# Gate's logits on VectorE instead of TensorE, for 17 of 18 token tiles

## The chip, the cores and the metric

One Trainium2 chip, of which one NeuronCore runs the program. The metric is the device time of one execution in microseconds (us). Kernel before: median 1043.26 us of three runs (1043.04 to 1044.56).

## The reference

Attention with a threshold under the row's maximum, then a dense ELU layer, then a mixture of experts with one expert for each token. All data are fp32. The change concerns the line that makes the logits.

```python
def _moe_ref(x, w_in, w_out):                       # x: 2304 tokens x 512, from the attention
    h = x @ w_in                                    # 2048 wide
    g = np.where(h > 0.0, h, np.exp(np.minimum(h, 0.0)) - 1.0)
    return g @ w_out                                # called x2 below
...
    logits = x @ w_gate + modality_bias[modality_id]     # x = x2; w_gate: 512 x 8
    e_idx = np.argmax(logits, axis=1)
    probs = softmax(logits)
    gate_w = probs[np.arange(N), e_idx]
    for e in range(E):                                   # 8 experts
        mask = e_idx == e
        out[mask] = gate_w[mask, None] * (np.maximum(x[mask] @ w1[e], 0.0) @ w2[e])
```

## The kernel before, in words

The program has three parts on one core. `Phase1` computes attention and, batch by batch, the ELU layer's first product; it writes g to memory (`gD`). `Phase2` computes that product for the last batch, unpacks `w_out` into `WB`, and then goes over 18 **token tiles** of 128 tokens (`tokens`, i = 0 to 17); this loop is where the change lies. `lead` starts the first expert there, and `Experts` runs all the others.

In both phases a planner (`Plan`) sets the order. Each step is `pl.op(engine, cost, due, function, deps, buffers)`; the planner simulates the engines with these costs, takes among the steps that are ready the one with the lowest due time, and so fixes one order of instructions for each engine. On the chip each engine keeps to that order: an instruction that waits holds up all that stand behind it. `STEP` is the distance of the due times of two tiles, in ns. The framework adds waits so that two engines aren't in the same PSUM tile at once.

One token tile i, before the change:

- `load`, `hi`, `lo`, twice (a half of 8 slices of g each): a DMA of 512 KB into `gr`, a cast on ScalarE (ACT) into `gs`, and on GpSimd (POOL) the rest `gs` = `gr` - cast. There are two `gs` buffers: a half's cast waits until PE is through with the half before the last.
- `mm`: 48 matmuls of 128x512 on TensorE (PE), 24 to a half, sum x2 in a PSUM tile `u`.
- `copy`: ACT copies x2 to `xrow`. `turn`: four PE transposes of `xrow` into the PSUM tile `xt`. `turned`: ACT copies that to `xw`. `logits`: `xw` times `w_gate` on PE, four matmuls in the source, each run as two.
- `top`: seven small VectorE (DVE) instructions, bias, maximum, one-hot `ohb`. `rank`: three small matmuls on PE count the earlier tokens of the same expert; they need `ohb`. `place`: eight DVE instructions make an address; `table`: an indirect DMA issued by POOL writes the token's number there. `neg`, `ex`, `gate`: DVE, ACT, DVE make the gate weight; `put` writes the row to memory.

After tile 8, `first` picks the fullest expert so far; `weights` then loads its eight pieces in turn through one staging buffer `stg`: DMA, cast on ACT, rest on POOL, into `WA`. After tile 14, `begun` makes the number `base`, which SP (the queue that issues the DMAs) loads; behind it in SP's order stands `idx` of `lead`, then POOL gathers 256 rows (`xg`), and PE turns them round (L829) inside tile 17.

Of the kernel before, what the change touches and what calls it, by code (L numbers as in the profile page):

```python
# [8 lines left out]
F32 = mybir.dt.float32  # L9
# [4 lines left out]
ALU = mybir.AluOpType  # L14
# [5 lines left out]
B, H, S, D = 4, 8, 576, 64  # L20
# [38 lines left out]
class Plan:  # L59
# [726 lines left out]


PREDICT, SNAP = 8, 14
STEP = 12700
EARLY = 128 * (PREDICT + 1)  # L790

BLOCKS = [TT] + [(EARLY // (k + 1) + (NT - EARLY) // k + 1 + 127) // 128 for k in range(1, E)]
# [263 lines left out]
class Phase2:  # L1056

    def __init__(self, tc, opt, ph, WA, WB, ident, w_out, mod, w_gate, bias, w1, w2, out, x2D, tabD):  # L1060
        self.tc, self.nc, self.opt, self.ph = tc, tc.nc, opt, ph
        self.ident, self.mod, self.w_gate, self.bias = ident, mod, w_gate, bias
        self.w1, self.w2, self.out, self.x2D, self.tabD = w1, w2, out, x2D, tabD
        self.WO = WB.rearrange("p s (k f) -> p s k f", k=FC)
        self.wsrc = w_out.bitcast(I32).rearrange("(k p) n -> p k n", p=128)
        self.gv = ph.gD.rearrange("k p s -> p k s")
        self.V = [WA, WB]
        self.T = ph.T
        self.pl = Plan(ph.pl)

    def pools(self, ctx, keep, xa, xb, tp):
        tc, pl = self.tc, self.pl
        self.xa, self.xb, self.tp = xa, xb, tp
        one = self.one = keep.enter_context(tc.tile_pool(name="k1", bufs=1))
        pool = lambda name, bufs, **k: ctx.enter_context(tc.tile_pool(name=name, bufs=bufs, reuse_waits="tile", **k))
        self.sm, self.wk = pool("msm", 3), pool("gwk", 2)
        self.pu, self.pc = pool("ps_u", 6, space=PSUM), pool("ps_c", 1, space=PSUM)
        for tag, n in dict(u=6, xt=1, pr=1, xw=2, eh=2, g=4, gr=2, gs=2, stg=1, xrow=3, ht=1).items():
            pl.ring(tag, n, tag in ("gs", "ht", "xw"))
        self.XT0 = one.tile([128, 2, KT, 256], F32R, name="xt0")  # L1080
        self.XG0 = one.tile([128, 2, XW], F32, name="xg0")
        self.IDX = [one.tile([128, 24], I32, name=f"idx{i}") for i in range(2)]
        self.GT = [one.tile([128, 2], F32, name=f"gt{i}") for i in range(2)]
# [96 lines left out]
    def gate_weights(self, d):  # L1180

        def load():
            self.wg = self.one.tile([128, KT, E], F32, name="wg")
            self.nc.sync.dma_start(self.wg, self.w_gate.rearrange("(k p) e -> p k e", p=128))

        self.k_wg = self.pl.dma(200, 1, d, load)

    def tokens(self, i, d):

        nc, pl, T, sm = self.nc, self.pl, self.T, self.sm  # L1190
        bU = pl.new("u")
        parts, ready = [], []
        for hf in range(2):
# [3 lines left out]
            n = 2 * i + hf  # L1197
# [21 lines left out]
        prev = None  # L1219
# [12 lines left out]
            prev = pl.op("PE", 1404, d + STEP // 2 * h, lambda f0=f0: mm(f0),  # L1232
                         [prev, *ready[2 * h:2 * h + 2]] + self.wdone[f0] + self.wdone[f0 + 1], [bU, parts[h]])
        self.k_mm = prev
        bX, bT, bW, bP = pl.new("xrow"), pl.new("xt"), pl.new("xw"), pl.new("pr")

        def copy():
            T["x", i] = self.wk.tile([128, XW], F32, name="xrow", tag="xrow", bufs=3)
# [6 lines left out]
                nc.tensor.transpose(T["xt"][:, 128 * k:128 * k + 128], T["x", i][:, 128 * k:128 * k + 128], self.ident)  # L1245

        def turned():
            if i < 2:
                T["xw", i] = self.xb.tile([128, KT, 128], F32, name="xw", tag=("xh", "xl")[i], bufs=1)
            nc.scalar.copy(T["xw", i % 2].rearrange("p k t -> p (k t)"), T["xt"])  # L1250

        def logits():
            for k in range(KT):
                nc.tensor.matmul(T["xt"][:, 0:E], T["xw", i % 2][:, k, :], self.wg[:, k, :], start=(k == 0), stop=(k == KT - 1))  # L1254

        def top():
            lg = T["lg", i] = sm.tile([128, E], F32, name="lg")
            nc.vector.tensor_tensor(lg, T["xt"][:, 0:E], self.bt[:, i, :], op=ALU.add)  # L1258
            mx = T["mx", i] = sm.tile([128, 4], F32, name="mx")
            nc.vector.tensor_reduce(mx[:, 0:1], lg, axis=AX.X, op=ALU.max)  # L1260
            t8 = sm.tile([128, E], F32, name="t8")
            nc.vector.scalar_tensor_tensor(t8, lg, mx[:, 0:1], self.d8, op0=ALU.is_ge, op1=ALU.mult)
            nc.vector.tensor_reduce(mx[:, 1:2], t8, axis=AX.X, op=ALU.max)
            oh = T["oh", i] = sm.tile([128, E], F32, name="oh")
            nc.vector.tensor_scalar(oh, self.d8, mx[:, 1:2], None, op0=ALU.is_equal)
            T["ohb", i] = sm.tile([128, E], BF16, name="ohb")
            nc.vector.tensor_copy(T["ohb", i], oh)
# [44 lines left out]
        if i == TT - 1:  # L1312
            d -= 15000
        k = pl.op("A", 478, d, copy, [prev], [bU, bX])
        k = pl.op("PE", 436, d + 700, turn, [k], [bX, bT])
        k = pl.op("A", 478, d + 1300, turned, [k] + (self.l1mm if i < 2 else []), [bT, bW])
        k = pl.op("PE", 880, d + 2000, logits, [k, self.k_wg], [bT, bW])
        kt = pl.op("D", 1200, d + 3000, top, [k, self.k_const, self.k_bias], [bT])
        kr = pl.op("PE", 60, d + 4300, rank, [kt, self.k_place], [bP])
        self.k_place = kp = pl.op("D", 1199, d + 4600, place, [kr], [bP])  # L1320
        self.k_table.append(pl.op("P", 1040, d + 5800, table, [kp, self.k_init], extra=2000))
# [324 lines left out]
```

## Time and profile before

| | |
|---|---|
| median of three runs | 1043.26 us |
| the profiled execution: its time, its span | 1040.67 us, 1038.7 us |
| PE busy | 987.1 us, 95% of the span |
| DVE busy | 633.5 us, 61% |
| ACT busy | 566.5 us, 55% |
| POOL busy | 472.2 us, 45% |
| PE clock granted | 0.988 of full speed |

How to read it: the shares are means over the whole program; the token tiles take about 532 to 770 us of the span. What an engine does there is read from the timeline and from tables of stretches below. Times within the profile are us from the start of the span.

### The profile page before, as it was taken

What the parts mean: (1) busy time and instruction counts of PE and PEld (TensorE: products, weight loads), DVE (VectorE), ACT (ScalarE), POOL (GpSimd) and SP (SyncE); (2) the same over time, 40 slices, a digit from 0 to 9 for tenths busy, and PEclk for the clock granted to TensorE, in tenths of its full rate; (3) what the DMA queues carried; (4) which work ended last, traced back from release to release, by engine and by line L of the source; (5) the groups of instructions that cost most, each with busy time, mean ns of one, the idle gap of its engine ahead of it and who ended that gap; (6) DMA issues with size and microseconds to landing.
All of it is one profiled execution on the core that took longest, in us unless ns stands there. A gap on an engine that the chain in (4) does not pass through costs nothing. (4 is left out here: it accounts for less than half of the span.)

```text
span 1038.7 us, 17784 instructions
## 1 busy us (share of the span) xinstructions
PE 987.1 (95%) x6241; PEld 864.3 (83%) x6241; DVE 633.5 (61%) x1574; ACT 566.5 (55%) x1183; POOL 472.2 (45%) x346
## 2 busy tenths in 40 slices
PE   8999899899999999998889999999999998999993
PEld 7666698899999999998778888877888897888982
DVE  6878899998989897856851222243444653464431
ACT  5777899899999999976762222333221211121000
POOL 3444787787667667541024444477523210211110
PEclk9999999999999999999999999999999999999997
DMA  5544454434424332116863333355312520441111
GB/s 174 152 121 128 118 152 132 123 117 118 131 88 123 99 111 70 59 64 199 227 211 113 105 104 103 114 153 172 112 41 83 200 65 24 141 122 53 41 44 25
DMA packets 107538, 117.75 MB, mean 113 GB/s; under 512 B 11920, under 2 KB 83872, under 8 KB 107426
## 3 DMA queue, kind: packets, MB, share of 16 engines
q1 hardware_dynamic: 102930, 104.00, 33.8%
q0 software_dynamic: 4496, 12.35, 3.9%
q8 instruction: 59, 0.97, 0.4%
q14 instruction: 53, 0.43, 0.1%
HBM read 80.36 MB, written 29.85 MB: 106 GB/s over the span
## 5 line engine op out<-in xcount | busy, mean ns | idle before, releaser
L1227 PE MATMUL u<-WB,gs 128*128 128x512 f32 x864 | 216.1, 402 | 3.7 <-POOL gs L1210 2.6
L1227 PEld LDWEIGHTS u<-WB,gs 128*128 128x128 f32 x864 | 158.4, 189 | 39.5 <-POOL gs L1210 3.7
L480 POOL TENSOR_TENSOR tl<-tf,th 128x512 fp32r<-128x512 f32 (+1 forms) x120 | 145.3, 1215 | 80.8 <-ACT tf L477 80.3
L715 PE MATMUL h<-xh,WA 128*128 128x288 f32 x768 | 172.4, 300 | 0.9 <-DVE g L734 0.5
L715 PEld LDWEIGHTS h<-xh,WA 128*128 128x128 f32 x768 | 128.8, 189 | 3.6 <-DVE g L734 1.9
L1210 POOL TENSOR_TENSOR gs<-gr,gs 128x1024 fp32r<-128x1024 f32 x36 | 87.1, 2420 | 95.2 <-ACT gs L1206 95.1
L419 DVE SCALAR_TENSOR_TENSOR p<-s,a,e 128x576 f32<-128x576 f32 x144 | 116.5, 813 | 19.5 <-ACT e L409 12.8
L397 DVE TENSOR_REDUCE a<-s 128x1 f32<-128x576 f32 x144 | 107.4, 753 | 16.4 <-PE s L386 14.1
L715 PE MATMUL h<-xl,WA 128*128 128x288 f32 x384 | 113.2, 295 | 0.0
L409 ACT ACTIVATE e<-s,a 128x576 f32<-128x576 f32 x144 | 106.8, 745 | 8.3 <-DVE a L397 6.4
L430 PE MATMUL h<-ident,p 128*128 128x128 f32 x576 | 87.8, 276 | 6.3 <-DVE p L419 4.9
L877 ACT CAST xtr<-px 128x512 fp32r<-128x512 f32 x16 | 9.4, 588 | 150.3 <-issue 85.2
L1258 DVE TENSOR_TENSOR lg<-xt,bt 128x8 f32<-128x8 f32 x18 | 3.0, 166 | 135.3 <-PE xt L1254 135.3
L820 POOL DMA_INDIRECT out<-o,idx x16 | 17.7, 1104 | 144.6 <-DVE o L932 101.3
L386 PE MATMUL s<-kh,QS 128*128 128x288 f32 x320 | 79.8, 331 | 1.4 <-DVE p L419 0.8
L430 PEld LDWEIGHTS h<-ident,p 128*128 128x128 f32 x576 | 68.8, 141 | 11.5 <-DVE p L419 4.7
L715 PEld LDWEIGHTS h<-xl,WA 128*128 128x128 f32 x384 | 72.6, 189 | 0.0
L386 PE MATMUL s<-kl,QS 128*128 128x288 f32 x320 | 69.1, 298 | 0.6 <-POOL kl L300 0.6
L1206 ACT CAST gs<-gr 128x1024 fp32r<-128x1024 f32 x36 | 37.8, 1049 | 56.5 <-issue 35.3
L471 ACT CAST th<-h 128x512 fp32r<-128x512 f32 (+1 forms) x120 | 64.0, 542 | 4.5 <-PE h L430 3.5
L477 ACT COPY tf<-h 128x512 f32<-128x512 f32 (+1 forms) x120 | 64.6, 546 | 1.4
L715 PE MATMUL u<-xh,WA 128*128 128x288 f32 x256 | 55.6, 306 | 8.6 <-DVE g L734 8.3
(207 smaller groups left out, 2083.7 us busy)
## 6 DMA issues: line engine op xcount, KB each, us to landing
gD<-g SPq DMA_DIRECT2D x128, 144.0 KB
gr<-gD SPq DMA_DIRECT2D x36, 512.0 KB
stg<-w SPq DMA_DIRECT2D x24, 512.0 KB
kr<-kP SPq DMA_DIRECT2D x30, 288.0 KB
w<-w_in SPq DMA_DIRECT2D x16, 512.0 KB
gr<-w_out SPq DMA_DIRECT2D x16, 512.0 KB
VR<-v SPq DMA_DIRECT2D x16, 320.0 KB
x2D<-xrow SPq DMA_DIRECT2D x18, 256.5 KB
```

The costliest lines, as they stand in the source:

```text
L386: nc.tensor.matmul(s[:, hf, 0:288], q, k[:, 288 * hf:288 * hf + 288], start=(m == 0), stop=(m == len(mm) - 1))
L397: nc.vector.tensor_reduce(T["a", i][:, 0:1], T["s", i][:, :, 0:288], axis=AX.XY, op=ALU.max, negate=True)
L409: nc.scalar.activation(e, T["s", i][:, :, 0:288], AF.Exp, bias=T["a", i][:, 0:1])
L419: nc.vector.scalar_tensor_tensor(p, T["s", i][:, :, 0:288], T["a", i][:, 1:2], T["e", i], op0=ALU.is_ge, op1=ALU.mult, accum_out=T["sums", ...
L430: nc.tensor.transpose(tp[:, 128 * c:128 * c + 128], pf[:, 128 * c:128 * c + 128], self.ident)
L471: a1 = op("A", ta(4), de, lambda src=src, dst=dst: nc.scalar.copy(dst("th"), src()), [k5], [bT])
L477: nc.scalar.copy(f[:, :, 0:w], src())
L480: nc.gpsimd.tensor_tensor(dst("tl"), T["tf", i, g][:, :, 0:w], dst("th").bitcast(F32), op=ALU.subtract)
L715: nc.tensor.matmul(T["h", key], self.WIN[:, s, kt, fc * 128:fc * 128 + 128], x[:, kt, q], start=(kt == 0 and j == 0), stop=(kt == KT - 1 a ...
L1206: nc.scalar.copy(T["gs", n % 2][:, 0], T["gr", n])
L1210: nc.gpsimd.tensor_tensor(g[:, 1], T["gr", n], g[:, 0].bitcast(F32), op=ALU.subtract)
L1227: nc.tensor.matmul(T["x2", i], T["gs", n][:, a, f % 8, :], self.WO[:, b, f, :], start=(f == 0 and j == 0), stop=(f == FC - 1 and j == 2))
```

## The change

For tiles 0 to 16 the logits no longer come from `turn`, `turned` and `logits`. Instead `dots` runs eight DVE instructions: each multiplies x2 as it lies in PSUM with one column of `w_gate`, writes the product to the PSUM tile `xt` (which nobody reads) and puts its sum in one column of `dots`. For that, `w_gate` transposed is loaded onto all 128 partitions by two broadcast DMAs of 1 MB (`wr`), into the place where the last batch's x had lain and where `xw` was before. Tile 17 keeps the old way, with a third `xrow` for `xw`. `STEP` goes from 12700 to 11700, and the due times of `top` and all behind it are 5000 ns later for the tiles with dots.

```diff
-STEP = 12700
+STEP = 11700
...
     def gate_weights(self, d):
...
+        def rows(j):
+            self.T["wr", j] = t = self.xb.tile([128, 4, DM], F32, name="wr", tag=("xh", "xl")[j], bufs=1)
+            src = self.w_gateT.rearrange("(j e) d -> j (e d)", e=4)[j:j + 1]
+            self.nc.sync.dma_start(t.rearrange("p e d -> p (e d)"), src.to_broadcast([128, 4 * DM]))
-        self.k_wg = self.pl.dma(200, 1, d, load)
+        self.k_wr = [self.pl.dma(4000, 1, d + 9000 + 6000 * j, lambda j=j: rows(j), self.l1mm, extra=1500) for j in range(2)]
+        self.k_wg = self.pl.dma(200, 1, d + 20000, load)
...
+        fast = i == TT - 1
...
         def turned():
-            if i < 2:
-                T["xw", i] = self.xb.tile([128, KT, 128], F32, name="xw", tag=("xh", "xl")[i], bufs=1)
-            nc.scalar.copy(T["xw", i % 2].rearrange("p k t -> p (k t)"), T["xt"])
+            T["xw"] = self.wk.tile([128, XW], F32, name="xrow", tag="xrow", bufs=3)
+            nc.scalar.copy(T["xw"][:, 0:DM], T["xt"])
...
+        def dots(e0):
+            if e0 == 0:
+                T["xt"] = self.pc.tile([128, 512], F32, name="xt")
+                T["dots", i] = sm.tile([128, E], F32, name="dots")
+            for e in range(e0, e0 + 2):
+                nc.vector.scalar_tensor_tensor(T["xt"], T["x2", i], 1.0, T["wr", e // 4][:, e % 4, :], op0=ALU.mult, op1=ALU.mult,
+                                               accum_out=T["dots", i][:, e:e + 1])
...
-            nc.vector.tensor_tensor(lg, T["xt"][:, 0:E], self.bt[:, i, :], op=ALU.add)
+            nc.vector.tensor_tensor(lg, T["xt"][:, 0:E] if fast else T["dots", i], self.bt[:, i, :], op=ALU.add)
...
         k = pl.op("A", 478, d, copy, [prev], [bU, bX])
-        k = pl.op("PE", 436, d + 700, turn, [k], [bX, bT])
-        k = pl.op("A", 478, d + 1300, turned, [k] + (self.l1mm if i < 2 else []), [bT, bW])
-        k = pl.op("PE", 880, d + 2000, logits, [k, self.k_wg], [bT, bW])
-        kt = pl.op("D", 1200, d + 3000, top, [k, self.k_const, self.k_bias], [bT])
+        if fast:
+            bW = pl.new("xrow")
+            k = pl.op("PE", 436, d + 700, turn, [k], [bX, bT])
+            k = pl.op("A", 478, d + 1300, turned, [k], [bT, bW])
+            k = pl.op("PE", 880, d + 2000, logits, [k, self.k_wg], [bT, bW])
+        else:
+            k = prev
+            for e0 in range(0, E, 2):
+                k = pl.op("D", 1380, d + 500 + 1300 * e0 // 2, lambda e0=e0: dots(e0), [k, self.k_wr[e0 // 4]], [bU, bT])
+            d += 5000
+        kt = pl.op("D", 1400, d + 3000, top, [k, self.k_const, self.k_bias], [bT])
...
+        "w_gateT": f(np.asarray(inputs["moe2_w_gate"]).T),
```

How the order changes. On PE, this is one tile of the middle of the loop before (L1227 the tile's matmuls, L1245 `turn`, L1254 `logits`, L1272 to L1274 `rank`):

```order
L1227 MATMUL u<-WB,gs 128x512 x30
L1245 MATMUL xt<-ident,xrow 128x128 x4
L1227 MATMUL u<-WB,gs 128x512 x6
L1254 MATMUL xt<-wg,xw 128x8 x4
L1227 MATMUL u<-WB,gs 128x512 x12
L1272 LDWEIGHTS U
L1272 MATMUL pr<-ohb,U 128x8
```

and the same place now (L1234 the tile's matmuls, L1288 to L1290 `rank`):

```order
L1234 MATMUL u<-WB,gs 128x512 x48
L1288 LDWEIGHTS U
L1288 MATMUL pr<-ohb,U 128x8
L1289 LDWEIGHTS ones
L1289 MATMUL pr<-ohs,ones 128x8
L1290 LDWEIGHTS ones
L1290 MATMUL pr<-eb,ones 128x8
```

`turn` and `logits` are gone, and the rank of tile i now stands exactly at the end of tile i+1; before it stood six matmuls ahead of that end.

On DVE, one tile of the middle before, from `top` (L1258) over `neg` and `gate` (L1296 to L1306) to `place` (L1277), with the engines that each waits for:

```order
L1258 TENSOR_TENSOR lg<-xt,bt 128x8 [waits PE_49,Activation_49]
L1260 TENSOR_REDUCE mx<-lg 128x1 [waits DVE_49]
...
L1267 CAST ohb<-oh 128x8 [waits DVE_49]
L1296 TENSOR_SCALAR mx<-mx 128x1
L1305 TENSOR_SCALAR mx<-mx 128x1 [waits Activation_49]
L1306 RECIPROCAL xrow<-mx 128x1 [waits DVE_49]
L1277 TENSOR_TENSOR ohs<-ohs,ohb 128x8 [waits PE_49]
```

and now, from the first dots (L1269) of a tile over `place` (L1293 to L1303) of the tile before it to `top` (L1274, L1276):

```order
L1269 SCALAR_TENSOR_TENSOR xt,dots<-u,wr 128x512 [waits PE_49]
L1269 SCALAR_TENSOR_TENSOR xt,dots<-u,wr 128x512 [waits DVE_49]
L1293 TENSOR_TENSOR ohs<-ohs,ohb 128x8 [waits PE_49]
L1296 SCALAR_TENSOR_TENSOR j_7966,rf<-pr,oh 128x8 [waits PE_49]
...
L1303 TENSOR_TENSOR ri<-ri 128x1 [waits DVE_49]
L1269 SCALAR_TENSOR_TENSOR xt,dots<-u,wr 128x512 [waits Activation_49]
L1269 SCALAR_TENSOR_TENSOR xt,dots<-u,wr 128x512 [waits DVE_49] x5
L1274 TENSOR_TENSOR lg<-dots,bt 128x8 [waits DVE_49]
L1276 TENSOR_REDUCE mx<-lg 128x1 [waits DVE_49]
```

Two of a tile's dots come first, then `place` of the tile before, then six more, the first of which waits for ACT's copy of x2 (that copy in turn waits for the first two dots), then `top`. The bias is now added to a tile of SBUF, no longer to one of PSUM.

On POOL, in the stage where the expert's weights are loaded, before (L1210 `lo`, L1378 the rest of the weights, L1290 `table`, here of tiles 11 and 12):

```order
L1290 DMA tabD<-ids,ri 32896x1 [waits DMASW2_49,DVE_49]
L1210 TENSOR_TENSOR gs<-gr,gs 128x1024 [waits DMAHW1_49,PE_49,Activation_49]
L1210 TENSOR_TENSOR gs<-gr,gs 128x1024 [waits DMAHW3_49,PE_49,Activation_49]
L1378 TENSOR_TENSOR WA<-stg,WA 128x1024 [waits DMAHW5_49,Activation_49]
L1290 DMA tabD<-ids,ri 32896x1 [waits DMASW3_49,DVE_49]
```

and now (L1217 `lo`, L1401 the weights, L1306 `table`, here of tiles 11 and 12):

```order
L1306 DMA tabD<-ids,ri 32896x1 [waits DMASW2_49,DVE_49]
L1401 TENSOR_TENSOR WA<-stg,WA 128x1024 [waits DMAHW5_49,Activation_49]
L1217 TENSOR_TENSOR gs<-gr,gs 128x1024 [waits DMAHW3_49,PE_49,Activation_49]
L1401 TENSOR_TENSOR WA<-stg,WA 128x1024 [waits DMAHW7_49,Activation_49]
L1306 DMA tabD<-ids,ri 32896x1 [waits DMASW3_49,DVE_49]
L1217 TENSOR_TENSOR gs<-gr,gs 128x1024 [waits DMAHW6_49,PE_49,Activation_49]
```

The table of a tile, which follows on its rank and place, has moved by one `lo`, except here: the table of tile 12 stands right ahead of the `lo` of tile 14's second half.

## Rows read from the trace of the kernel before

**Rows 1.** Stretches: us, busy time (and count) of each engine, granted clock, DMA:

```profile
546.00:660.50 114.50, 114.50 (x560) 92.69 (x559) 22.84 (x153) 31.16 (x54) 51.67 (x26) 1.00 0.34 102
660.50:770.40 109.90, 107.05 (x524) 85.67 (x524) 43.94 (x168) 35.74 (x57) 65.02 (x33) 1.00 0.42 130
```

**Rows 2.** Timeline of PE, one tile: start, length, instruction, count:

```profile
621.79 0.18 PE L1272 MATMUL pr<-ohb,U 128*128 128x8 bf16 x1
...
622.03 7.29 PE L1227 MATMUL u<-WB,gs 128*128 128x512 f32 x30
629.16 0.60 PE L1245 MATMUL xt<-ident,xrow 128*128 128x128 f32 x4
629.51 1.64 PE L1227 MATMUL u<-WB,gs 128*128 128x512 f32 x6
630.99 0.95 PE L1254 MATMUL xt<-wg,xw 128*128 128x8 f32 x8
631.80 3.06 PE L1227 MATMUL u<-WB,gs 128*128 128x512 f32 x12
```

**Rows 3.** Timeline of PE: first tiles, two ranks, the end of tile 17:

```profile
535.22 16.66 PE L1227 MATMUL u<-WB,gs 128*128 128x512 f32 x70 [1.73 <-POOL gs L1210]
...
557.25 0.18 PE L1272 MATMUL pr<-ohb,U 128*128 128x8 bf16 x1
...
660.50 0.18 PE L1272 MATMUL pr<-ohb,U 128*128 128x8 bf16 x1
...
770.43 1.60 PE L836 MATMUL u<-xt,WA 128*128 128x256 f32 x12
```

**Rows 4.** Timeline of ACT and POOL: cast and rest of a half:

```profile
624.22 1.05 ACT L1206 CAST gs<-gr 128x1024 fp32r<-128x1024 f32 x1
625.36 2.42 POOL L1210 TENSOR_TENSOR gs<-gr,gs 128x1024 fp32r<-128x1024 f32 x1 [0.77 <-ACT gs L1206]
```

**Rows 5.** One DVE line: count, shortest, median and longest in ns, first and last:

```profile
L878 DVE TENSOR_TENSOR xtr<-px,xtr x16: 690/692/692, 811.2 to 1000.4; 128x512 fp32r<-128x512 f32 x16
```

**Rows 6.** Timeline of DVE in the attention: product with a sum, what follows:

```profile
302.95 0.81 DVE L419 SCALAR_TENSOR_TENSOR p<-s,a,e 128x576 f32<-128x576 f32 x1
...
303.81 0.37 DVE L536 TENSOR_TENSOR th<-h,th 64x64 fp32r<-64x64 f32 x2
```

**Rows 7.** Timeline of DVE, top to place of a tile:

```profile
657.87 0.17 DVE L1258 TENSOR_TENSOR lg<-xt,bt 128x8 f32<-128x8 f32 x1 [8.72 <-PE xt L1254]
...
659.03 0.17 DVE L1267 CAST ohb<-oh 128x8 bf16<-128x8 f32 x1
...
661.88 0.16 DVE L1287 TENSOR_TENSOR ri<-ri 128x1 int32<-128x1 int32 x1
```

**Rows 8.** Timeline of POOL and DVE, a tile's place in the weights stage:

```profile
674.52 2.40 POOL L1378 TENSOR_TENSOR WA<-stg,WA 128x1024 fp32r<-128x1024 f32 x1 [2.97 <-ACT WA L1377]
...
675.04 1.90 DVE L1277 TENSOR_TENSOR ohs<-ohs,ohb 128x8 bf16<-128x8 bf16 x1
...
677.88 0.16 DVE L1287 TENSOR_TENSOR ri<-ri 128x1 int32<-128x1 int32 x1
```

**Rows 9.** Timeline of ACT: the cast of one piece of the weights:

```profile
680.88 1.05 ACT L1377 CAST WA<-stg 128x1024 fp32r<-128x1024 f32 x1 [3.84 <-DMA stg<-w]
```

**Rows 10.** Timeline of DVE, POOL and PE: from base to the turned rows:

```profile
746.73 0.14 DVE L1435 TENSOR_SCALAR base<-fl 1x1 int32<-1x1 f32 x1
...
750.22 0.99 POOL L816 DMA_INDIRECT xg<-x2D,idx  x1 [3.91 <-issue]
...
755.19 0.98 PE L829 MATMUL u<-ident,xg 128*128 128x128 f32 x7
```

**Rows 11.** Stretches: a broadcast of 64 rows alone; loads of g alone:

```profile
462.00:464.00 2.00, 2.00 (x17) 2.00 (x17) 0.39 (x1) 0.86 (x2) 0.00 (x0) 1.00 0.43 147
538.00:540.00 2.00, 2.00 (x10) 1.59 (x9) 0.80 (x3) 0.93 (x3) 1.31 (x1) 1.00 1.03 348
```

**Rows 12.** Waits of PE from 545 to 800: total, times, longest:

```profile
PE pr L1272 <- DVE mx L1296: 1.4, 1, 1.4
```

More of the change, by code (lines that the diff above doesn't have):

```diff
@@ L1056, with __init__ @@
 class Phase2:
-    def __init__(self, tc, opt, ph, WA, WB, ident, w_out, mod, w_gate, bias, w1, w2, out, x2D, tabD):
+    def __init__(self, tc, opt, ph, WA, WB, ident, w_out, mod, w_gate, w_gateT, bias, w1, w2, out, x2D, tabD):
         self.tc, self.nc, self.opt, self.ph = tc, tc.nc, opt, ph
-        self.ident, self.mod, self.w_gate, self.bias = ident, mod, w_gate, bias
+        self.ident, self.mod, self.w_gate, self.w_gateT, self.bias = ident, mod, w_gate, w_gateT, bias
         self.w1, self.w2, self.out, self.x2D, self.tabD = w1, w2, out, x2D, tabD
@@ L1077, in pools @@
         self.pu, self.pc = pool("ps_u", 6, space=PSUM), pool("ps_c", 1, space=PSUM)
-        for tag, n in dict(u=6, xt=1, pr=1, xw=2, eh=2, g=4, gr=2, gs=2, stg=1, xrow=3, ht=1).items():
-            pl.ring(tag, n, tag in ("gs", "ht", "xw"))
+        for tag, n in dict(u=6, xt=1, pr=1, eh=2, g=4, gr=2, gs=2, stg=1, xrow=3, ht=1).items():
+            pl.ring(tag, n, tag in ("gs", "ht"))
         self.XT0 = one.tile([128, 2, KT, 256], F32R, name="xt0")
@@ L1234, in tokens @@
         self.k_mm = prev
-        bX, bT, bW, bP = pl.new("xrow"), pl.new("xt"), pl.new("xw"), pl.new("pr")
+        bX, bT, bP = pl.new("xrow"), pl.new("xt"), pl.new("pr")
+        fast = i == TT - 1
         def copy():
@@ L1247, in turned @@
         def turned():
-            if i < 2:
-                T["xw", i] = self.xb.tile([128, KT, 128], F32, name="xw", tag=("xh", "xl")[i], bufs=1)
-            nc.scalar.copy(T["xw", i % 2].rearrange("p k t -> p (k t)"), T["xt"])
+            T["xw"] = self.wk.tile([128, XW], F32, name="xrow", tag="xrow", bufs=3)
+            nc.scalar.copy(T["xw"][:, 0:DM], T["xt"])
         def logits():
             for k in range(KT):
-                nc.tensor.matmul(T["xt"][:, 0:E], T["xw", i % 2][:, k, :], self.wg[:, k, :], start=(k == 0), stop=(k == KT - 1))
+                nc.tensor.matmul(T["xt"][:, 0:E], T["xw"][:, 128 * k:128 * k + 128], self.wg[:, k, :], start=(k == 0), stop=(k == KT - 1))
+        def dots(e0):
[5 more added lines that the diff above has]
+                                               accum_out=T["dots", i][:, e:e + 1])
         def top():
             lg = T["lg", i] = sm.tile([128, E], F32, name="lg")
-            nc.vector.tensor_tensor(lg, T["xt"][:, 0:E], self.bt[:, i, :], op=ALU.add)
+            nc.vector.tensor_tensor(lg, T["xt"][:, 0:E] if fast else T["dots", i], self.bt[:, i, :], op=ALU.add)
             mx = T["mx", i] = sm.tile([128, 4], F32, name="mx")
@@ L1578, in run, with core @@
             pl.emit()
-def core(tc, qP, kP, qF, kF, v, tau, w_in, w_out, mod, w_gate, bias, w1, w2, out):
+def core(tc, qP, kP, qF, kF, v, tau, w_in, w_out, mod, w_gate, w_gateT, bias, w1, w2, out):
     nc = tc.nc
@@ L1600, in core @@
             WB = wb.tile([128, 2, 8192], F32R, name="WB")
-            l2 = Phase2(tc, OPT, ph, WA, WB, ident, w_out, mod, w_gate, bias, w1, w2, out, x2D, tabD)
+            l2 = Phase2(tc, OPT, ph, WA, WB, ident, w_out, mod, w_gate, w_gateT, bias, w1, w2, out, x2D, tabD)
             with ExitStack() as p2:
```

## The prediction

> **What bounds the kernel now.** I read the shares first, then a table of stretches over the token tiles, then PE's timeline in one tile, then who waits for whom. In the nine tiles up to the rank of tile 8 PE is busy for the whole stretch at full clock, while DVE has 22.84 of 114.50 us, ACT 31.16 and POOL 51.67 [rows 1]. So a tile lasts as long as PE's own instructions. The rank of one tile to that of the eighth behind it is 660.50 - 557.25 = 103.25, or 12.906 us for a tile [rows 3]. Its parts: 48 matmuls at 0.2377 us (30 of them from 622.03 to `turn` at 629.16) are 11.41, `turn` is 629.51 - 629.16 = 0.35, `logits` 631.80 - 630.99 = 0.81, `rank` 622.03 - 621.79 = 0.24 [rows 2]; together 12.81, so there is 0.1 of gaps.
>
> The late stage, in which the expert's weights come in, is no longer pure PE: in 109.90 us PE is busy 107.05, POOL 65.02 and DVE 43.94 [rows 1]. Of all ranks one waited for DVE, 1.4 us [rows 12]. The frame: tile 1 ends 0.24 + 6 x 0.2377 = 1.67 behind its rank at 557.25, at 558.92, so tile 0 ends near 546.0; tile 17 ends at 770.43 [rows 3]. Those 224.4 us are what the change can alter; before and behind them the order is the same, and I take their lengths as unchanged.
>
> **What is removed.** `turn` and `logits` go from 17 tiles. A tile on PE is then 48 x 0.2377 + 0.24 = 11.65 us. 17 of them are 198.05; the transposes of the gathered rows (seven within 0.98, which spans some matmuls; I take 0.8 [rows 10]) and a count of 0.1 make 198.95. Against 224.4 that is **-25.4 us** if PE never waits: 17 x (12.906 - 11.65) = 21.3 of removed work, and some 4.1 that the late stage now loses (2.85 of it idle [rows 1]).
>
> **What is added on DVE.** Eight dots a tile. No row shows DVE write PSUM with a sum. The nearest are a 512 wide sum of a PSUM operand, 0.692 us [rows 5], and a product with a sum 576 wide, of which the next instruction starts 303.81 - 302.95 = 0.86 behind it [rows 6]. 576 to 512 scales the second to 0.76. I take a spacing of 0.74; the rows bound it by 0.69 and 0.86, and the cost of a second PSUM access could be above both (a rival below). Eight are 5.92 us. With `top` (657.87 to 659.20, 1.33), `neg` and `gate` (some 0.8) and `place` (1.2) [rows 7, 8] DVE has some 9.3 us of work in a tile of 11.65. It fits, but it is now a chain.
>
> [...]
>
> **The new wait and what is queued behind it.** In the order now, `rank` of tile i stands on PE exactly at the end of tile i+1, with all matmuls of tile i+2 behind it. It needs `ohb`, hence all eight dots and `top`. Times from a tile's end, T = 0, for the middle of the loop: the first two dots 0.28 to 1.76. Meanwhile ACT's cast (1.05) and POOL's `lo` (2.42) [rows 4] run, `lo` from 1.42 to 3.84. `place` of the tile before comes next on DVE, and its first instruction has two SBUF operands. Such an instruction is held while POOL runs a sum: at 675.04 it took 1.90 us, until 676.94, where POOL's 2.40 from 674.52 end [rows 8]. So `place` gets away at 3.84 and ends 1.12 later (677.88 + 0.16 - 676.94 [rows 8]), at 4.96. Six dots end at 9.40. The half of the next tile ends at 0.24 + 24 x 0.2377 = 5.94, and its buffer's refill puts `lo` on POOL from 7.36 to 9.78. The bias sum of `top`, which now reads two SBUF tiles (before, PSUM), is held until 9.78; `ohb` is there 1.15 later (659.20 - 657.87 less its 0.17 [rows 7]), at 10.93. PE wants it at 11.65. **Slack 0.7 us, so tiles 1 to 8 cost nothing**; the cover is lost once the spacing s exceeds 0.87, since then the dots and not POOL come last.
>
> **The late stage, tiles 9 to 16.** Here POOL also runs eight weight pieces of 2.40. A piece follows the one before by at least 3.84 + 1.05 + 2.40 = 7.3 us [rows 8, 9], so about one falls in each tile, and POOL has 2 x 2.42 + 2.40 + 0.99 (the table, priced by the gather's issue [rows 10]) = 8.2 of 11.65. A piece that stands between `lo` and a held DVE instruction pushes `ohb` back by up to 2.4; less the slack of 0.7, a bad meeting costs up to 1.7 to 2. I laid the orders of DVE, ACT, POOL and PE beside each other with the durations above and followed each tile. Stalls of PE at ranks: tile 9 0.5, tile 10 0.95, tile 11 1.95, tile 12 1.0, tile 13 none, tile 14 0.75, tile 15 2.2 (the five small instructions up to `base`, some 0.6, now stand ahead of its `top`). Stalls for `lo`: tiles 12 and 16 0.6 and 0.45, and tile 14's second half 2.7. There `table` of tile 12 stands ahead of the `lo`: `place` ends at 4.96, the table takes 1.0, `lo` 2.42, with three gaps of some 0.1 that is 8.7, and PE wants it at 5.94. Last the gathered rows: `base` at 746.73 to the turn at 755.19 is a chain of 8.5 us [rows 10], and `base` moves from about 5 us behind tile 15's end to about 11 behind, so the turn inside tile 17 is late by about 1.7. Sum **+12.8 us**. Each of these hangs on which instruction meets which, so I give the sum the bounds 4.1 (as much as before loses) and 20.
>
> **The start.** The two broadcasts (2 MB into SBUF) go out on SP ahead of the third load of g. Loads of g alone move 348 GB/s, a broadcast of 64 rows alone 147 [rows 11]. At 348 they take 6 us of the queues and PE does not notice, since two buffers are ahead; at 147 they take 14, and tile 1's matmuls would wait some 7 us. I put +1 (about what 250 GB/s gives), bounds 0 and 7. [...]
>
> **Sum.** -25.4 + 12.8 + 1 = -11.6 us. The profiled execution would go from 1040.67 to 1029.1. That execution stands 2.6 below the median of three, 1043.26, so for the median I say **1032 us** (1043.26 - 11.6 = 1031.7). About 2.1 us, 0.2%, is what a measurement of this kernel can tell from no change.
>
> **Rivals.**
> First, the late stage takes it: the stalls meet less badly than I followed them, because a late PE also gives POOL and DVE time, and it loses only the 4.1 of before. Then -25.4 + 4.1 + 0 = -21.3, about **1022**. For it speaks that only one rank waited for DVE before [rows 12]; against it that now every tile has 0.7 of slack and a piece is 2.4.
> Second, slow start and bad meetings together: 7 for the broadcasts at 147 GB/s and 15 to 16 late, -25.4 + 22.5 = -3, about **1040**. The one broadcast in the trace speaks for it [rows 11]; against it, it fills 64 rows and not 128, and had little to move.
> Third, the other side: the dots are dear. If writing the product to PSUM while reading x2 from PSUM raises s, a tile is bound by DVE: `place` ends at 4.96, then six dots, then 1.32 of `top` to `ohb` and 0.1 of gaps, so from rank to rank 6.4 + 6 s. Above s = 0.87 that exceeds 11.65, at 1.08 the 12.9 of before; with the late stage's extra 8.7 (12.8 - 4.1) and the start's 1 the kernel is slower from 17 x (6.4 + 6 s - 12.9) + 9.7 = 0, s = 0.99. At s = 1.2 a tile is 13.6: 17 x 0.7 = 12, with the 9.7 some 22 if nothing overlaps; about **1060**. No row has such an s; both nearest ones lie below 0.87.
> Fourth, nothing comes of it: s between 0.96 and 1.02, or stalls that just eat the 25.4, within 2 us of **1043**.
>
> **How the numbers follow.** The forecast of 1032 with its own range of 1027 to 1037: 0.45. First rival 0.26, second 0.15, third 0.10, fourth 0.04. The range reaches from 1021, the case of few stalls, to 1042, the slow start; it leaves out the third, the fourth in part, and the edges. Faster: 0.45 + 0.26 + most of the second, 0.83; same 0.05; slower 0.12.
>
> **What the profile after would show.** Right: the spacing of L1269 at 0.70 to 0.80; ranks in tiles 1 to 8 at 11.65 with no wait of PE; `ohs` (L1293) and `top`'s first instruction (L1274) stretched to 2 us and more, ending with POOL's `lo`; in tiles 9 to 16 waits of PE at L1288 for DVE and for `gs`, the longest ahead of tile 14's second half; ranks some 12.5 to 13 apart there; tile 17 ending near 759. Wrong: a spacing above 0.87 would turn the middle of the loop from PE's bound to DVE's; a PE wait of several us for `gs` within the first three tiles would be the broadcasts; no waits in the late stage would be the first rival. An `lg` sum that isn't held by POOL would take the lock out of my chain, leaving 1 us more slack.

## The result, and the profile after

The changed kernel takes 1031.72 us, the median of four executions (1027.41 to 1032.66); before, 1043.43 (1043.04 to 1044.56, four executions). The ratio is 0.9878, 95% interval 0.9849 to 0.9907: 11.7 us less, where 1032 was said. The profiled execution took 1027.41 us, span 1025.2, against a span of 1038.7 before. It is the fastest of the four; the other three had a mean granted clock of 0.981 to 0.983 against its 0.986.

PE's timeline in the middle of the loop, the rows that answer to [rows 2] and [rows 3]:

```profile
615.18 0.18 PE L1288 MATMUL pr<-ohb,U 128*128 128x8 bf16 x1
...
615.42 11.51 PE L1234 MATMUL u<-WB,gs 128*128 128x512 f32 x48
626.77 0.18 PE L1288 MATMUL pr<-ohb,U 128*128 128x8 bf16 x1
...
756.75 1.70 PE L836 MATMUL u<-xt,WA 128*128 128x256 f32 x12
```

From rank to rank it is 626.77 - 615.18 = 11.59 us, all 48 matmuls in one run. Tile 17 ends at 756.75, before at 770.43.

Stretches from the end of tile 1 to the rank of tile 8, and from 660.50, just ahead of the rank of tile 9, to the end of tile 17, against [rows 1] (us, busy time and count of PE, PEld, DVE, ACT, POOL, granted clock, DMA):

```profile
557.22:649.96 92.74, 92.74 (x409) 73.36 (x409) 82.07 (x273) 24.62 (x40) 46.35 (x24) 1.00 0.38 114
...
660.50:756.70 96.20, 86.48 (x375) 67.15 (x373) 83.88 (x254) 29.02 (x46) 58.73 (x30) 0.98 0.49 137
```

In the first PE has no gap, though DVE now has 82 of 93 us; between the two it has none either. In the second PE is idle for 9.7 us. Who it waits for there (engine, line; total, times, longest):

```profile
PE pr L1288 <- DVE mx L1312: 5.7, 5, 2.1
PE u L1234 <- POOL gs L1217: 2.1, 1, 2.1
PE u L829 <- DMA xg<-x2D,idx: 2.0, 2, 1.2
```

The account, from the end of tile 1 (its rank, 557.22) to the end of tile 17 (756.75): 199.53 us. Sixteen times 11.59 are 185.4, the turn of the gathered rows and two counts 1.0; 13.1 are lost. The waits above are 9.7 of these (from the rows of the timeline), the lower clock behind one of them 1.6 (0.64 granted from 709.50 to 713.00 and 0.86 from there to 716.30: 22 matmuls from 709.48 to the rank at 716.27, 6.8 us, where 22 of the middle, at a clock of 1.00 and 11.35 for 48, take 5.2; the row is in the last section), and the rest falls behind the waits and is not followed further. Before, the same stretch took 770.43 - 558.92 = 211.5 (tile 1's end worked out in the prediction). So 12.0 us come from here and 1.7 from tile 1, whose end moved from 558.92 to 557.22.

### The profile page after: what moved, and what is told of

It is laid out like the page before. It is cut to its first block, busy times and chain, and to the rows that moved or that the text cites. A ratio compares the mean times of both kernels' runs of the same rounds, so it can differ in the third digit from the quotient of the medians.

```text
span 1025.2 us, 17626 instructions
## 1 busy us (share of the span) xinstructions
PE 966.1 (94%) x6037; PEld 843.8 (82%) x6037; DVE 751.9 (73%) x1846; ACT 558.5 (54%) x1166; POOL 471.0 (46%) x346
## 5 line engine op out<-in xcount | busy, mean ns | idle before, releaser
L1234 PE MATMUL u<-WB,gs 128*128 128x512 f32 x864 | 209.4, 401 | 4.3 <-POOL gs L1217 3.8
L1234 PEld LDWEIGHTS u<-WB,gs 128*128 128x128 f32 x864 | 162.1, 190 | 43.7 <-POOL gs L1217 4.7
L1217 POOL TENSOR_TENSOR gs<-gr,gs 128x1024 fp32r<-128x1024 f32 x36 | 86.1, 2393 | 110.8 <-ACT gs L1213 110.6
L1269 DVE SCALAR_TENSOR_TENSOR xt<-u,wr 128x512 f32<-128x512 f32 x136 | 94.8, 697 | 9.0 <-PE u L1234 2.6
```

What stands on the lines that cost most here:

```text
L1217: nc.gpsimd.tensor_tensor(g[:, 1], T["gr", n], g[:, 0].bitcast(F32), op=ALU.subtract)
L1234: nc.tensor.matmul(T["x2", i], T["gs", n][:, a, f % 8, :], self.WO[:, b, f, :], start=(f == 0 and j == 0), stop=(f == FC - 1 and j == 2))
L1269: nc.vector.scalar_tensor_tensor(T["xt"], T["x2", i], 1.0, T["wr", e // 4][:, e % 4, :], op0=ALU.mult, op1=ALU.mult, accum_out=T["dots", i ...
```

## The experiments

Executions of one kernel differ by up to 7 us, part of it ahead of the stretch that is compared here: the rank of tile 0 started between 556.9 and 563.3 in the profiles. What a kernel does in the tiles is therefore read from its profile: **the stage**, from tile 1's end (in these profiles the rank of tile 0; where that stands 1.43 us later, 1.43 are added) to the first L836, and **the late tile**, a sixth of the way from the rank of tile 9 to that of tile 15.

| kernel | median, us | ratio, 95% interval | stage | late tile |
|---|---|---|---|---|
| before | 1043.43 | | 211.5 | 13.57 |
| changed | 1031.72 | 0.9878 (0.9849 to 0.9907) | 199.5 | 13.33 |
| sums in PSUM | 1033.21 | 0.9888 (0.9867 to 0.9908) | 199.1 | 13.25 |
| products in SBUF | 1034.85 | 0.9906 (0.9882 to 0.9931) | 201.5 | 13.38 |
| table moved | 1038.71 | 0.9937 (0.9914 to 0.9961) | 205.9 | 13.43 |
| 12 dots | 1053.76 | 1.0084 (1.0057 to 1.011) | 223.1 | 14.27 |
| pieces small | 1022.44 | 0.977 (0.9755 to 0.9786) | 189.6 | 11.73 |
| rank later | 1033.35 | 0.9886 (0.9865 to 0.9907) | 201.7 | 13.25 |
| place later | 1040.38 | 0.9951 (0.9937 to 0.9964) | 209.7 | 13.72 |
| idx ahead of base | 1031.01 | 0.9852 (0.9836 to 0.9867) | 197.7 | 13.42 |
| sums in halves | 1029.04 | 0.9866 (0.9842 to 0.9889) | 200.3 | 13.44 |
| halves, idx | 1028.90 | 0.9851 (0.9829 to 0.9874) | 199.2 | 13.48 |
| quarters, idx | 1027.60 | 0.985 (0.9823 to 0.9878) | 200.3 | 12.75 |
| quarters, idx, two places | 1026.90 | 0.9822 (0.9803 to 0.9841) | 198.0 | 12.78 |

(The ratios go by the kernel before, run on the same chip each time.)

The stage is read from one execution of each kernel, and what the clock does in it is part of it. In the changed kernel 22 matmuls took 6.95 us where the granted clock was 0.64 and 0.86; with the sums in PSUM, where it was 1.00, the same 22 took 5.42. In most of these kernels one or two stretches of the late matmuls take some 1 to 2.5 us longer (48 matmuls 13.0 instead of 11.5), mostly behind a wait of 1.7 to 3.8 us; that the clock is behind these too is read from the lengths alone. The changed kernel has one such stretch, "idx ahead of base" two, "place later" four, "pieces small" none. So a difference of 1 to 2 us between two stages doesn't show by itself what an edit is worth.

Two theories were set against each other first. **A**: late ranks wait because the bias sum of `top`, the only instruction that the change itself gave a second SBUF operand, is held by POOL. **B**: DVE has too much work. They gave way to **C**: DVE with whatever holds it is the bound in the late stage, and the hold comes from the weight pieces on POOL.

**Sums in PSUM.** The product goes to SBUF, the sum of each dot to PSUM.

```diff
-                T["dots", i] = sm.tile([128, E], F32, name="dots")
+                T["dots", i] = T["xt"][:, 0:E]
+                T["sb"] = self.wk.tile([128, 512], BF16, name="sbp", tag="sbp", bufs=1)
...
-                nc.vector.scalar_tensor_tensor(T["xt"], ...
+                nc.vector.scalar_tensor_tensor(T["sb"], ...
```

> The changed kernel with two places exchanged: the product of each dot goes to an SBUF tile (bf16), its sum to PSUM, so that the bias sum at the head of top reads PSUM plus SBUF again instead of two SBUF tiles; the orders of all engines are as in the changed kernel. Theory A (late ranks wait because the first sum of top is held while POOL runs a sum): its instances of 1.40 to 3.67 us fall to about 0.2, the waits of PE at the ranks fall from 5.7 us to 1.5 to 2.5, and the time falls by 2.5 to 4 us. Theory B (DVE simply has too much work in a tile, 10 of 11.6 us): the sum is still stretched or the dots end later, the waits at the ranks stay within 1 us of 5.7, no change of time.

The stage fell by 0.5 us only, the waits at ranks to 4.6; the wait at rank 12 is gone, but the 48 matmuls ahead of it took 13.05 us instead of 11.51. DVE's timeline of this kernel at one late `top`:

```profile
703.09 0.17 DVE L1275 TENSOR_TENSOR lg<-xt,bt 128x8 f32<-128x8 f32 x1
703.29 0.16 DVE L1277 TENSOR_REDUCE mx<-lg 128x1 f32<-128x8 f32 x1
703.48 0.54 DVE L1279 SCALAR_TENSOR_TENSOR t<-lg,mx,d 128x8 f32<-128x8 f32 x1
...
704.25 2.15 DVE L1282 TENSOR_SCALAR oh<-d,mx 128x8 f32<-128x8 f32 x1
```

The bias sum is free (0.17), as A says, but two of the next instructions are held in its place, one behind the other: the 0.54 (0.23 where free) ends at 704.02, where POOL's 2.39 from 701.60 end at 703.99, and the 2.15 (0.23 where free) at 706.40, where POOL's 2.41 from 703.96 end at 706.37. So A's instruction was held, and freeing it alone gives nothing: the hold is passed on. From the rank of tile 9 to that of tile 15 the DVE instructions beside the dots that took over 0.3 us (most are free at 0.14 to 0.23) add up to 25.1 us in the changed kernel and to 25.6 here. B is not shown by this either.

**Products in SBUF.** The product goes to `sb` as above, but the sum stays in `dots` in SBUF.

> The changed kernel with only the product of each dot going to an SBUF tile (bf16) instead of PSUM; the sum stays in SBUF. It prices the write into PSUM and is the control of the kernel with the sums in PSUM. If the write to PSUM costs something, the spacing of the dots falls from 0.79 to about 0.74 or less and every top is 0.4 us earlier; if not, it stays at 0.79. With theory A the bias sum is still held in the late stage and the waits at the ranks stay at 5 to 6 us; time within 1.5 us of the changed kernel. If the dot itself were now held by POOL (its output and second operand in SBUF), dots of 1 us and more would show and the time would rise by 5 us or more.

Dots now stand 0.73 apart (608.13 to 608.86) against 0.79 in the changed kernel, and 0.79 where the sum goes to PSUM. So PSUM on the output side, for the product or for the sum, cost 0.06 a dot here. Dots that end 0.4 us sooner did not help: the stage was 2 us longer, with waits of 5.8 at the ranks and two stretches of longer matmuls (48 in 12.91, and 30 in 8.15 where the changed kernel has 7.27); the time, 3 us above the changed kernel's, was expected within 1.5. No dot was held by POOL (0.67 to 0.69 us each, the read of the sum not counted).

**Table moved.**

```diff
-        self.k_table.append(pl.op("P", 1040, d + 5800, table, ...
+        self.k_table.append(pl.op("P", 1040, d + 8800, table, ...
```

> The changed kernel with the due time of table 3000 ns later. The only instruction that moves is the table of tile 12, which now stands behind the rest of the half (lo) that PE waited for 2.09 us; all else is in the same order. If the stall hangs on that one place: the wait for gs inside tile 13's matmuls goes from 2.09 to 0 to 1.1, the 1.7 us lost after it at a clock of 0.64 go too, and the time falls by 2.5 to 4 us. If the lo is late because POOL is full (pieces of the weights), the wait stays above 1.5 us and the time does not move.

(The matmuls meant there are those of tile 14.) The wait for `gs` in its place is gone, and the kernel is slower: ratio 0.9937. PE's timeline:

```profile
716.61 0.17 PE L1288 MATMUL pr<-ohb,U 128*128 128x8 bf16 x1 [2.18 <-DVE mx L1312]
...
730.63 0.17 PE L1288 MATMUL pr<-ohb,U 128*128 128x8 bf16 x1 [2.28 <-DVE mx L1312]
...
752.55 0.33 PE L829 MATMUL u<-ident,xg 128*128 128x128 f32 x1 [3.81 <-DMA xg<-x2D,idx]
```

In the changed kernel the ranks of tiles 13 and 14 waited 0 and 0.58. What the table gave, the next two ranks took back. The 3.81, and the longer matmuls behind it (30 in 9.29 us, 7.27 in the changed kernel), have a cause of their own:

```profile
749.17 0.98 POOL L816 DMA_INDIRECT xg<-x2D,idx  x1 [7.87 <-DMA x2D<-xrow]
```

By the profile the gather waited for the write of tile 15's rows (`put`), though it gathers rows of tiles up to 14; in the changed kernel that write, at 748.74, came behind the gather, at 743.67. Here the write was issued at 744.89, behind `idx` at 743.59.

**12 dots.** Every other dot is issued twice.

```diff
-            for e in range(e0, e0 + 2):
+            for e in (e0, e0, e0 + 1):
```

> The changed kernel with every other dot issued twice, 12 per tile instead of 8, as if a dot cost 1.19 us; the result is the same. This prices the rival in which dear dots make the kernel slower. By that rival's formula a tile is 6.4 + 6 x 1.19 = 13.5 us against 11.59, the middle of the loop is bound by DVE with no idle time there, and the time is 1031.7 + 17 x 1.9 = 1064, less what the late stalls lose to it, 1055 to 1064. If the chain overlaps better than the formula (only DVE's own work counts: 12 x 0.79 + 1.3 + 1.2 + 0.8 = 12.8 a tile), 1031.7 + 17 x 1.2 less some 8 = about 1044 to 1052.

```profile
603.10 0.17 PE L1288 MATMUL pr<-ohb,U 128*128 128x8 bf16 x1 [1.62 <-DVE mx L1312]
...
643.12 0.17 PE L1288 MATMUL pr<-ohb,U 128*128 128x8 bf16 x1 [1.60 <-DVE mx L1312]
```

In the middle a tile takes 13.34 us (these two ranks are three tiles apart), near the 13.5 of the rival's formula and above the 12.8 of the work alone. One of the three tiles took 13.05 us for its 48 matmuls, the others 11.51, and lasted no longer: there PE did not wait at the rank. (The granted clock was 0.97 as a mean from 563.06 to 669.88, in which two tiles were of that kind.) The median rose by 22, to 1053.76, which lies between the two forecasts of the time. So the rival's price of a tile was right, its time a little too high, and 0.79 is far from the spacing it needs.

**Pieces small.** POOL's rest of each weight piece covers 64 of 1024 columns.

```diff
-            self.V[0][:, 1, sl], T["stg", c], self.V[0][:, 0, sl].bitcast(F32), ...
+            self.V[0][:, 1, sl][:, 0:64], T["stg", c][:, 0:64], self.V[0][:, 0, sl][:, 0:64].bitcast(F32), ...
```

> The changed kernel in which GpSimd's rest of each weight piece covers 64 of 1024 columns (the other columns of the low part are left as they lie, so the first expert's product is not exact); DMAs, casts and all orders stay. From the rank of tile 0 to the head of lead the changed kernel takes 199.5 us, and from the rank of tile 9 to that of tile 15 13.33 a tile, against 11.59 in the middle of the loop. Theory C (in the late stage DVE with what holds it is the bound: the pieces on POOL hold place and top): without pieces 11.6 to 12.0 a tile, the stage 188 to 192, the time 7 to 11 us less. Rival D (the weights' DMAs and ACT's casts, or the loads of g behind them, make the stage slow): 13 and more a tile still, stage within 3 us of 199.5.

The late tiles, stretch from the rank of tile 9 to that of tile 15:

```profile
666.30:736.70 70.40, 69.96 (x308) 54.97 (x307) 62.92 (x210) 25.73 (x40) 37.18 (x26) 1.00 0.68 172
```

PE is busy 69.96 of 70.40, with all the weights' DMAs and casts in place (172 GB/s). A late tile takes 11.73, no rank waits, and DVE's instructions over 0.3 us, counted as above, fall from 25.1 to 14.2 us. This shows C's cause, POOL's sums for the pieces, and rules out D. How much of the loss is DVE being held and how much is `lo` standing behind a piece on POOL, this run doesn't separate.

**Rank later.** Six matmuls into the next tile.

```diff
-            prev = pl.op("PE", 1404, d + STEP // 2 * h, lambda f0=f0: mm(f0),
+            prev = pl.op("PE", 1404, d + STEP * f0 // FC, lambda f0=f0: mm(f0),
...
-        kr = pl.op("PE", 60, d + 4300, rank, ...
+        kr = pl.op("PE", 60, d + 4300 + (0 if fast else 2500), rank, ...
```

> The changed kernel with the due times of a tile's matmuls spread and the rank's due time later, so that each rank stands six matmuls (1.43 us) into the next tile instead of at its head. If the picture in the prediction is right, in which each rank has a slack of its own, every rank wait falls by 1.43: 5.7 us in five waits to about 0.7, stage 199.5 to about 195, time 4 to 5 us less. By theory C the ranks, places and tops form a chain on DVE from tile to tile that does not care where PE stands: 13.3 a tile remains, only the first wait gives 1.4 once, and the stage falls by 0 to 2 us.

Waits of PE in this kernel:

```profile
PE u L1234 <- POOL gs L1217: 5.4, 3, 3.5
PE u L829 <- DMA xg<-x2D,idx: 3.3, 2, 2.2
PE pr L1288 <- DVE mx L1312: 0.8, 1, 0.8
```

The ranks waited 0.8 as the prediction's picture has it, and the stage grew by 2.2: the same time is now lost at `gs` and `xg`. Theory C was right that a late tile doesn't get shorter (13.25) and wrong on the stage, which it had at 0 to 2 us less. It is not DVE alone: the later rank makes a later `place`, a later `table`, and a later `lo` behind it on POOL.

**Place later.** Behind six dots of the next tile instead of two.

```diff
                 k = pl.op("D", 1380, d + 500 + 1300 * e0 // 2, lambda e0=e0: dots(e0), ...
+                if e0 == 4 and i:
+                    pl.ops[self.kp][4].add(k)
```

> The changed kernel with place of a tile behind six of the next tile's dots instead of two (a dependency added for the planner; the counts and tables move with it, and idx comes ahead of base on SP). Theory C: place then meets POOL between two of its sums, so that in the middle of the loop ohs falls from 1.94 to about 0.2 (no time won there, PE is the bound), and in the late stage 1.7 us and more of held time a tile goes: 11.8 to 12.6 a tile, the stage 190 to 196, time 4 to 9 us less. If the holds only move on to other instructions, as they did when the sums went to PSUM: 13.0 to 13.5 a tile, stage within 2 us of 199.5.

C's forecast failed, and so did the other (a stage within 2 us of 199.5): the stage is 10 us longer. `ohs` did fall to 0.16, but `top` is now held 2.24 in every tile of the middle:

```profile
593.57 2.24 DVE L1274 TENSOR_TENSOR lg<-dots,bt 128x8 f32<-128x8 f32 x1
...
602.89 0.16 DVE L1293 TENSOR_TENSOR ohs<-ohs,ohb 128x8 bf16<-128x8 bf16 x1
```

```profile
592.35 0.98 POOL L1306 DMA_INDIRECT tabD<-ids,ri  x1 [3.60 <-DVE ri L1303]
593.37 2.40 POOL L1217 TENSOR_TENSOR gs<-gr,gs 128x1024 fp32r<-128x1024 f32 x1
```

The table, later too, pushed `lo` right under `top`. A tile of the middle went from 11.59 to 12.07 and a late one to 13.72; four stretches of longer matmuls in the stage (48 in 13.05 and in 13.04, 30 in 8.83, 24 in 7.61), some 1.6 us each, are in this too.

**Idx ahead of base.** A dependency for the planner, so that SP issues `idx` before it loads `base`.

```diff
         k = pl.dma(100, 1, d - 20000, idx, [self.k_e0] + snap)
+        pl.ops[self.k_b1][4].add(k - 1)
```

> The changed kernel with only one thing exchanged on SP: the load of the index (idx, L812) stands ahead of the load of base (L1461), which it does not need. If base is what makes the gathered rows late, as the prediction has it: idx goes out at the landing of tile 14's table, some 2 to 3 us earlier, PE's waits for xg (2.0 us) go to 0, and the stage falls by 1.5 to 2.5 us. If the table or the row writes are what the gather waits for, the waits stay at 1.5 to 2.5.

As forecast: the wait for `xg` is gone, the stage 1.8 us shorter. The time alone would not show it: the interval of the ratio overlaps that of the changed kernel. PE at that place:

```profile
752.16 1.07 PE L829 MATMUL u<-ident,xg 128*128 128x128 f32 x8
```

**Sums in halves.** Both kinds of POOL's sums as two of 512 columns (`lo` shown).

```diff
-                nc.gpsimd.tensor_tensor(g[:, 1], T["gr", n], ...
+                for a in (0, 4):
+                    nc.gpsimd.tensor_tensor(g[:, 1, a:a + 4], T["gr", n][:, a:a + 4], ...
```

> The changed kernel in which each sum of 1024 columns on GpSimd (lo of a half, rest of a weight piece) is issued as two of 512 columns one behind the other; order and work are the same. Theory C (a DVE instruction is held until POOL's running sum ends and gets in at the end of an instruction): no hold is longer than about 1.2 us, ohs in the middle falls from 1.94 to about 0.7, the late stage from 13.33 to about 12.4 to 12.9 a tile, the stage from 199.5 to 193 to 197. If a hold lasts as long as POOL has sums behind one another, whatever their length, holds stay as they are and the stage within 1.5 us of 199.5.

In the middle `ohs` falls from 1.94 to 0.94, since it gets in between two halves, but `ri` (L1302), which was free (0.16), is then held 0.69 by the second half:

```profile
616.38 2.55 POOL L1218 TENSOR_TENSOR gs<-gr,gs 128x512 fp32r<-128x512 f32 x2 [3.08 <-ACT gs L1213]
```

```profile
616.77 0.94 DVE L1294 TENSOR_TENSOR ohs<-ohs,ohb 128x8 bf16<-128x8 bf16 x1
...
618.26 0.69 DVE L1302 TENSOR_TENSOR ri<-ri 128x1 int32<-128x1 int32 x1
```

Each hold lasted to the end of a running half, as C says: `ohs` ends at 617.71, the first half of POOL's 2.55 at about 617.66, `ri` at 618.95, the second half at 618.93. The gain does not follow, because an instruction further on in the chain is held again: DVE's instructions over 0.3 us, counted as above, add up to 28.1 us, against 25.1. Stage and late tile are not shorter (200.3 and 13.44).

**Halves and idx.**

> The two together: sums on GpSimd in halves of 512 columns, and on SP the load of the index ahead of the load of base. By theory C the two gains lie at different places and add: the stage 191 to 195.5, the time 1024 to 1029. If late stalls only move, as in the kernels with the table and the place moved: within 2 us of the kernel with base alone, 1031.0.

The stage of 199.2 is that of the changed kernel, 1.1 below the halves alone: idx gave part of its 1.8, the halves nothing. So the gains did not add in the stage, where 191 to 195.5 was forecast. The time doesn't decide between the two: 1028.90 is at the edge of the one forecast and 2.1 us from the other.

**Quarters and idx.** As before, with 256 columns.

> As the kernel with halves and the index ahead of base, but GpSimd's sums in quarters of 256 columns. By theory C holds of at most 0.65 us, 11.9 to 12.4 a tile in the late stage, the stage 189 to 193, the time 1022 to 1027; this is near the 189.6 us of the kernel with hardly any weight piece on POOL. What speaks against it: what each GpSimd instruction costs beside its columns, and if DVE's getting in delays POOL, lo ends later and the waits move to gs; then no better than the halves.

DVE's instructions over 0.3 us fall to 18.0 us, a late tile to 12.75, and the ranks wait 1.8 in all; `xg` and `gs` now wait 3.7 and 2.6, with longer matmuls behind both (30 in 9.13 where the changed kernel has 7.27, 22 in 6.96), so the stage is 200.3 and the forecast of 189 to 193 failed. Four quarters take 2.82 us where one sum took 2.40.

**Quarters, idx and two places.** With the table moved as above, and the turn of the gathered rows 12 and 18 matmuls later.

> The kernel with GpSimd's sums in quarters and the index ahead of base, with two more places moved: the table of tile 12 behind lo of tile 14's second half (as in the kernel with the table moved), and the turn of the gathered rows 12 and 18 matmuls later inside tile 17. In the kernel with quarters the waits left are gs 2.3 (and 1.7 after it at the lower clock), xg 3.7 (and 0.8), ranks 1.8, in a stage of 200.3. If with short holds a removed wait stays removed: the turn's 4.5 go in full, of the table's 4.0 some 2 to 4: the stage 191.5 to 194, the time 1018 to 1023. If the ring of DVE, POOL and PE gives the table's wait back at the next ranks, as with whole sums: only the turn's 4.5 go, stage 195 to 197, time 1022 to 1025.

The turn's wait went from 3.7 to 0.6. The waits for `gs` rose from 2.6 to 6.7, so the stage fell by 2.3, less than either forecast. POOL is busy 17.60 of 20 us at the worst place:

```profile
700.00:720.00 20.00, 17.80 (x76) 13.71 (x76) 15.21 (x53) 6.61 (x9) 17.60 (x25) 1.00 0.63 176
```

This is the fastest of the kernels that do all the work, 1026.9 us; its interval ends at 0.9841, just below the 0.9849 where that of the changed kernel begins.

## Why the prediction was right, step by step

**Removed work.** -25.4 was right in kind and 1 us short: a tile is 11.59, not 11.65. The 48 matmuls take 11.35 us (615.42 to 626.77), not 11.41; the rank takes the 0.24 that was said.

**Dots.** 0.79 us apart, taken as 0.74, inside the bounds 0.69 to 0.86. The rows of the changed kernel:

```profile
705.68 0.69 DVE L1269 SCALAR_TENSOR_TENSOR xt<-u,wr 128x512 f32<-128x512 f32 x1
706.29 0.14 DVE L1269 DVE_READ_ACCUMULATOR xt<-u,wr 128x1 f32 x1
706.47 0.70 DVE L1269 SCALAR_TENSOR_TENSOR xt<-u,wr 128x512 f32<-128x512 f32 x1
```

The main part alone takes 0.69, and the read of the sum, 0.14, ends 0.06 behind it.

**The chain of a tile.** Right in the middle for `place`: `ohs` is held 1.94 to the end of POOL's sum, and no rank of tiles 0 to 8 waits.

```profile
616.31 2.40 POOL L1217 TENSOR_TENSOR gs<-gr,gs 128x1024 fp32r<-128x1024 f32 x1 [3.21 <-ACT gs L1213]
616.78 1.94 DVE L1293 TENSOR_TENSOR ohs<-ohs,ohb 128x8 bf16<-128x8 bf16 x1
...
622.30 2.39 POOL L1217 TENSOR_TENSOR gs<-gr,gs 128x1024 fp32r<-128x1024 f32 x1 [1.21 <-ACT gs L1213]
624.48 0.23 DVE L1274 TENSOR_TENSOR lg<-dots,bt 128x8 f32<-128x8 f32 x1
```

Not right for `top`: its bias sum was to be stretched to 2 us and took 0.23 here, since at a spacing of 0.79 the dots end almost as late as `lo`; only in the late tiles was it held, up to 3.67. Two slips in the working have no effect on the sum: the 1.12 of `place` is 1.10 by its own rows, and with 4.96 + 6 s = 9.78 the dots come last from s = 0.80 on, while 0.87 is where the slack is gone.

**Late stage.** Said 12.8, lost 13.1. Place by place, said and measured: rank 9 0.5 and 0, rank 10 0.95 and 0.48, rank 11 1.95 and 2.12, rank 12 1.0 and 1.31, rank 13 0 and 0, rank 14 0.75 and 0.58, rank 15 2.2 and 1.19, `lo` of tile 14 2.7 and 2.09, the two smaller `lo` 1.05 and 0, gathered rows 1.7 and 1.95. That is 9.7 of waits; the sum fits because what the terms overstate is made up by losses that they left out: 1.6 at the lower clock (0.64 and 0.86), and some 1.8 behind the waits. That the sum comes out is luck, then; that the late stage takes half of what was removed is not.
What the prediction did not say is that these terms are not independent. It treated each as a stall that could be taken away; the kernels with the table, rank and place moved fit a late stage that is a ring (`rank` to `place` to `table` to `lo` to matmuls, and `place` to dots to `top` to `rank`), in which a tile takes 13.2 to 13.7 us whichever instruction waits, as long as POOL's sums are whole. The ring itself is a reading of these runs. Only less work on POOL (pieces small) shortened the late tile without a loss elsewhere.

**Start.** Said +1, was 0. In the stretch of the broadcasts (532 to 535):

```profile
532.00:535.00 3.00, 0.86 (x3) 0.30 (x2) 1.55 (x1) 2.50 (x6) 2.32 (x1) 1.00 1.09 381
```

DMA moved 381 GB/s, and the 94 matmuls of tiles 0 and 1 ran through in 22.28 us. The low bound of 147 GB/s did not apply to these transfers. This is the profiled execution. In the profiles of six other kernels that begin alike (sums in PSUM, products in SBUF, 12 dots, pieces small, rank later, place later) the matmuls of tiles 0 and 1 took 1.5 to 2.6 us longer, and in three (table moved, pieces small, idx ahead of base) PE waited 0.2 to 0.8 for `gs` in tile 1. Whether the broadcasts have a part in that was not tried.

**Rivals.** The late stage did not take the stalls (first), the broadcasts were not slow (second), and the dots cost 0.79 (third); that dear dots would have turned the sign was shown by 12 dots, 1.0084. The fourth, that nothing comes of it, is excluded by the interval, 0.9849 to 0.9907.

**The number.** In the profiles the span fell by 13.5 us where 11.6 was said, and the profiled execution took 1027.41 where 1029.1 was said. That the median came out at 1031.72, against 1031.7, is luck in part: the profiled execution before lay 2.6 us below its median, the one after 4.3.

## What to carry to other kernels

Moving work to an engine that has room by its busy share can still make a chain of it: here PE came to wait 5.7 us at the ranks. Follow the instructions of one period in order, and count the time for which another engine's instruction holds each (`ohs` 1.94 us, to the end of POOL's sum) as part of its own. In the late stage here, taking one wait away moved it (table moved: the waits at the ranks went from 5.7 to 9.6 us); look for the work in the ring that can be made less (pieces small: a late tile of 11.73 against 13.33). Cutting POOL's sums into halves didn't help by itself, since many DVE instructions were held in turn (28.1 us of them over 0.3 us, against 25.1).

## What the runs showed of the hardware that was not expected

Not only sums of two SBUF tensors were held while POOL ran a sum: a TENSOR_SCALAR that reads one SBUF tile and a scalar for each partition took 2.15 us (0.23 free) with the sums in PSUM, and in the kernel "halves, idx" the cast of `oh` to bf16 took 1.20 (0.17 free), to 704.37, where POOL's 2.53 from 701.81 end at 704.34. The two reductions with the sums in PSUM, at 703.29 and 704.06, with POOL in a sum too, were not (0.16).

The clock fell behind a wait of 2.09 us in the changed kernel, from 1.00 (700 to 707) to 0.64 of full speed as a mean of 709.50 to 713.00; a wait of 1.31 had ended 8.7 us before that one did.

```profile
709.48 6.95 PE L1234 MATMUL u<-WB,gs 128*128 128x512 f32 x22 [2.09 <-POOL gs L1217]
```

In the kernel with the sums in PSUM, where no wait stood at rank 12, a wait of 2.10 at the same place left the clock at 1.00 (714 to 722), and the 22 matmuls took 5.42. The earlier wait does not explain this: with idx ahead of base none stood at rank 12 either, and behind a wait of 1.89 the 22 matmuls took 6.96, near the 6.95 of the changed kernel.

```profile
714.69 6.96 PE L1234 MATMUL u<-WB,gs 128*128 128x512 f32 x22 [1.89 <-POOL gs L1217]
```

In both of these kernels the 48 matmuls of the tile before had taken longer too (13.05 and 13.03), so that does not tell them apart. What decides it stays open.
